# An attention and feed-forward kernel: emission order by measured durations, paced weights, and one weight group more kept in DRAM

## The chip, the cores and the metric

The kernel runs on one core of a Trainium2 chip. The metric is the device time of one execution in microseconds, as the median over several runs. TensorE is PE in the profile, VectorE is DVE, ScalarE is ACT, GpSimd is POOL, and SP is the queue from which nearly all transfers are issued.

## What is computed

Three stages follow one another, over 4 batches of 448 tokens with 768 features:

```
attn = sigmoid(q @ k.T / 8 - log(448));  x = attn @ v          # 12 heads of 64
xk, xr = mu * x + (1 - mu) * x_prev                            # x_prev: one token back
x = sigmoid(xr @ w_r) * (relu(xk @ w_k)**2 @ w_v)              # 768 -> 1024 -> 768
u = x + real(fft over tokens and features of x)
un = (u - mean(u)) / sqrt(var(u) + 1e-6)
out = u + relu(un @ w_ch1) @ w_ch2                             # 768 -> 3072 -> 768
```

## The kernel before

**Precision.** The products of the feed-forward layers are made of three matmuls each: every operand is split into a high and a low part (names that end in `h` and `l`), and high by high, high by low and low by high are added up. The weights arrive as 64-bit floats. `load_split` loads such a piece raw, rebuilds a 32-bit float from its words on DVE (one `ts`, three `stt`, one product), and then writes the high part (a cast) and the low part (a subtraction). In the first stage DVE does all of it, in halves of 128 x 384; a half is seven DVE instructions.

**Stages.** Attention goes by 24 pairs of heads. `scores(i)` makes 7 score products of pair i, `weigh` applies the sigmoid on ACT and writes `sg`, `attnv(i)` multiplies with `v`, and `join` copies the result to `x` (ACT), stores it in DRAM and mixes it with the token before it: `mix` on ACT, `stt` on DVE, a cast to `xkh` on ACT, a subtraction to `xkl` on DVE. Six pairs are one batch. Once a batch's six pieces and the weights `wk` are there, `keys` makes its 8 key tiles of 18 matmuls, between the pairs that are still to come. Behind them lie the receptance (`r`, 4 x 6 tiles of 18 matmuls, on `xr`, the same mix with `mu_r`, read back from DRAM), the values (`v`), into which the Fourier transform of each batch is worked (`pa`, `qa`, `pq`, then a mean `mu` and a variance `var`), and the feed-forward network (`f`): 12 weight groups g by 4 batches, `ffn1(g, b)` 36 matmuls and `ffn2(g, b)` 36. It needs `un`, the split of the centred rows of a batch: `load_k2` makes those of batches 0 and 1, `load_un` those of 2 and 3.

**What sets the order.** Every engine runs its own list in order, and the lists are fixed when the program is built. `Order` keeps a planned clock `o.now` and lets generators emit instructions: each asks in planned time whether what it needs is done (`need`, `issued`), and the cost functions `mm`, `tt`, `stt`, `ts`, `act` and `dma` say how long an instruction is taken to last. These costs move no work and have no effect on the chip but through the order. A key, value or feed-forward matmul waits in `o.feed` and is emitted when no generator is due. `attention` starts a pair every `PACE` us of planned time while there is something in `o.feed`.

**Weights of the first stage.** Two lanes (`first_weights`) start at planned 10 and 13 us, each takes one half of the columns of `wk`, `wr` and the first group of `w1` and `w2`, with one raw buffer. The split first group goes to DRAM (`w0_d`) and comes back by `load_first`. Stage one ends when those stores are issued.

Of the kernel before, what the change touches and what calls it, by code (L numbers as in the profile page):

```python
# [12 lines left out]
F32 = mybir.dt.float32  # L13
# [17 lines left out]
PACE = 11.0  # L31
# [63 lines left out]
class Order:  # L95
# [33 lines left out]

    def run(self, until=None):  # L130

        while until is None or until not in self.at:
# [65 lines left out]
    def stt(self, out, a, scalar, c, op0, op1):  # L198
        self.nc.vector.scalar_tensor_tensor(out, a, scalar, c, op0=op0, op1=op1)  # L199
        return self.spend(self.nc.vector, 0.13 + self.size(out) * 0.00104)  # L200

    def ts(self, out, a, s0, s1, op0, op1):
        self.nc.vector.tensor_scalar(out, a, s0, s1, op0=op0, op1=op1)
        return self.spend(self.nc.vector, 0.07 + self.size(out) * 0.00053)

    def act(self, out, a, fn=None, **kw):
# [4 lines left out]
        return self.spend(self.nc.scalar, 0.05 + self.size(out) * 0.00094)  # L211

    def dma(self, out, src, eng=None):
# [3 lines left out]
        self.free["dma"] = start + b / 4.0 / 220e3  # L217
# [3 lines left out]
def build(tc, ap):  # L221
# [10 lines left out]
    def load_split(pl, parts, gap=0.0, raws=1, lane=0, eng=None, vector=False):  # L232


        def load(src, hi, lo, key):
            n = o.size(hi)
            if not ap["wide"]:
                raw = pl.tile([128, n], F32, tag=f"wst{lane}", name="_".join(map(str, key)), bufs=1)
                return raw, o.dma(raw, src)
# [4 lines left out]
        for i, (wait, src, hi, lo, key) in enumerate(parts):  # L244
            yield from o.issued(*wait)
            raw, t = nxt or load(src, hi, lo, key)
            nxt = None
            ahead = parts[i + 1][1:] if i + 1 < len(parts) and all(k in o.at for k in parts[i + 1][0]) else None
            yield t
            n = o.size(hi)  # L250
# [30 lines left out]
            yield o.now  # L281
# [6 lines left out]
    w0_d = {nm: [dram.tile([128, 2, D], F32, name=f"{nm}0_d{i}") for i in range(2)] for nm in ("w1", "w2")}  # L288
# [39 lines left out]
    def weigh(i, n, ps):  # L328
        sg = att.tile([128, S], F32, tag="sg", name=f"sg_{i}_{n}", bufs=2 * len(places) + 1)
        o.at["sg", i, n] = t = o.act(sg, ps[:, 0:S], AF.Sigmoid, bias=bias_s, scale=1.0 / math.sqrt(DH))  # L330
        sg_t[i, n] = sg
        yield t

    def scores(i):
        k, q = pair_t["k", i], pair_t["q", i]
        for n, (c, j) in enumerate(places):
            ps = ps2.tile([128, 512], F32, tag="sc", name=f"sc_{i}_{n}")
            me = slice(0, 128) if j is None else slice(64 * j, 64 * j + 64)
            o.mm(ps[:, 0:S], k[me, c], q[me], True, True, 0.752 if j is None else 0.376)
            o.spawn(weigh(i, n, ps), o.now + 0.2)  # L340
        o.at["pair", i] = o.now

    def attnv(i, ps):
        v = pair_t["v", i]
        for n in [*range(1, len(places)), 0]:
            c, j = places[n]
            sg = sg_t.pop((i, n))
            if j is None:
                o.mm(ps[:, 0:S], v[:, c].rearrange("p j d -> p (j d)"), sg, False, True, 0.752, skip=True)
            else:  # L350
                me = slice(64 * j, 64 * j + 64)
                o.mm(ps[me, 0:S], v[:, c, j], sg, c == 0, False, 0.376, skip=True)
# [30 lines left out]
    def attention():  # L383
        for i in range(len(pairs) + 1):
            t0 = o.now
            if i < len(pairs):
# [3 lines left out]
                scores(i)  # L390
            if i > 0:
# [3 lines left out]
                attnv(i - 1, bank(f"av_{i - 1}"))  # L395
# [35 lines left out]
    w_parts = [[], []]  # L431
    for f in range(NF + KD):
# [4 lines left out]
        for i in range(2):  # L437
            cs = slice(D // 2 * i, D // 2 * i + D // 2)
            w_parts[i].append(((), src[:, cs], hl[0][:, cs], hl[1][:, cs], (*key, i)))

    def first_weights(lane):

        n = D // 2
        cs = slice(n * lane, n * lane + n)
        yield from load_split(att, w_parts[lane], lane=lane, vector=True)
        for nm in ("w1", "w2"):
            for i in range(2):
                t = att.tile([128, 2, n], F32R, tag=f"first{lane}", name=f"{nm}0_{i}_{lane}", bufs=1)
                yield from load_split(att, [((), ap[nm][i, :, cs], t[:, 0], t[:, 1], ("first", nm, i, lane))], lane=lane, vector=True)
                yield o.at["first", nm, i, lane]  # L450
                o.at["w0_d", nm, i, lane] = o.dma(w0_d[nm][i][:, :, cs], t.bitcast(F32))
# [9 lines left out]
    for i in range(2):  # L461
        o.run(("w0_d", "w2", 1, i))
# [40 lines left out]
    def receptance():  # L503
        for b in range(B):
# [13 lines left out]
    o.spawn(mixes())  # L518
    o.run(("key", B - 1))
# [13 lines left out]
    def load_k2():  # L533
# [10 lines left out]
        for n, (nm, b, i) in enumerate(places):  # L544
            if n >= NK:
# [8 lines left out]
            yield o.now + (0.2 if "receptance" in o.at else 4.0)  # L554
# [13 lines left out]
    o.spawn(load_split(wrp, wv_parts, 0.3, raws=2))  # L568
    o.spawn(receptance())
# [265 lines left out]
    def load_first(nm, pl):  # L835

        ts = w_t[nm, 0] = [
            [pl.tile([128, D], F32R, tag=nm + t, name=f"{nm}{t}0_{i}", bufs=2) for t in "hl"] for i in range(2)
        ]
        for i in range(2):  # L840
            for c, t in enumerate(ts[i]):
                t = o.dma(t.bitcast(F32), w0_d[nm][i][:, c])
            o.at.update(((nm, 0, i, c), t) for c in range(3))

    load_first("w1", wq)
# [12 lines left out]
    def load_un(pl, b):  # L858
# [9 lines left out]
        acc[b] = np_.tile([128, KD, S], F32, tag="x2", name=f"acc{b}", bufs=3)  # L868
# [56 lines left out]
    def out_done(g, b, e, ps):  # L925
        a = acc[b][:, e]
# [60 lines left out]
    load_first("w2", wpa)  # L987
# [7 lines left out]
    acc[1] = unb.tile([128, KD, S], F32, name="acc1")  # L995
# [69 lines left out]
```

## Time and profile before

| what | value |
|---|---|
| three runs | 1284.35, 1282.6, 1283.6 us; median 1283.6 |
| profiled execution, its own time | 1283.99 us |
| its span in the trace | 1282.2 us |
| mean granted clock of TensorE | 0.991 of 2.4 GHz |
| PE busy | 1253.4 us, 98% of the span |
| DVE busy | 737.7 us, 58% |
| ACT busy | 420.4 us, 33% |
| moved by DMA | 157.22 MB, mean 123 GB/s |

The span is that of the trace, 1.8 us shorter than the execution's own time. A row of a timeline has a start in us, a length in us, the engine and line, the operation, and in brackets the idle time before it with what released it. Line numbers are those of the kernel before; those of helpers (L157 for every matmul) say little, so names of tiles are read instead. A float32 product (scores, `av`) counts as two matmul records, and pipelined matmuls overlap in the records.

### The profile page before, as it was taken

To read this page: it belongs to the slowest core of one execution; us is meant where nothing else is said; L and a number is where in the kernel's file an instruction comes from. 1 tells how busy PE (TensorE), PEld (TensorE's weight loads), DVE (VectorE), ACT (ScalarE), POOL (GpSimd) and SP (SyncE) were. 2 spreads that over 40 slices of the span, in tenths; PEclk is the share of its full clock that TensorE was granted. 3 is DMA by queue.
4 is the path that set the end of the run, shared out by engine and by line. 5 is a ranking of instruction groups with operands and counts; after the bars stand their busy time and mean duration, and the time that the engine had idled before them with its cause. 6 is when DMAs were issued, how large, how long until landed. Compare 5 with 4: busy or idle time off the path is not lost.

```text
span 1282.2 us, 15838 instructions
## 1 busy us (share of the span) xinstructions
PE 1253.4 (98%) x6112; PEld 1062.6 (83%) x6112; DVE 737.7 (58%) x1280; ACT 420.4 (33%) x730; POOL 146.1 (11%) x125
## 2 busy tenths in 40 slices
PE   8789999999999999999999999999999999999998
PEld 3246466679888999998999999999999999999998
DVE  4999543123853476787545646564555546565554
ACT  6455666655642112335421212121211112121100
POOL 0000000000000000000111111011111111011486
PEclk9889999999998999999999999999999999999999
DMA  6666765325883644541321202111211112021344
GB/s 202 199 190 195 249 205 179 114 95 189 296 286 131 223 167 161 176 136 68 103 75 50 70 29 75 50 61 38 75 50 50 50 50 75 26 73 50 99 136 160
DMA packets 62763, 157.22 MB, mean 123 GB/s; under 512 B 7584, under 2 KB 33632, under 8 KB 62560
## 3 DMA queue, kind: packets, MB, share of 16 engines
q1 hardware_dynamic: 62016, 153.81, 35.9%
q0 software_dynamic: 672, 2.40, 0.6%
q8 instruction: 48, 0.79, 0.3%
q14 instruction: 27, 0.22, 0.1%
HBM read 113.56 MB, written 42.62 MB: 122 GB/s over the span
## 4 chain that ended last, share of the span: by engine, by line
PE 86%; DVE 10%; ACT 2%; issue 1%; DMA 1%; SPq 0%; DVEq 0%; ACTq 0%
PE f L157 54%; PE k L157 7%; PE v L157 7%; PE r L157 6%; PE sc L157 4%; PE av L157 4%; PE pq L157 1%; DVE wk_bits L199 1%; DVE wr_bits L199 1%; DMA k_d<-kp 1%; DVE x L191 1%; PE qa L157 1%; PE pa L157 1%; DVE wk L199 1%; DVE wk L191 0%
## 5 line engine op out<-in xcount | busy, mean ns | idle before, releaser
L157 PE MATMUL f<-un,w1h 128*128 128x448 f32 x1152 | 329.4, 366 | 1.4 <-DVE un L191 1.4
L157 PEld LDWEIGHTS f<-un,w1h 128*128 128x128 f32 x1152 | 216.5, 188 | 19.5 <-DVE un L191 2.5
L191 DVE TENSOR_TENSOR acc<-acc,f 128x448 f32<-128x448 f32 x264 | 163.0, 619 | 87.7 <-PE f L157 84.8
L157 PE MATMUL f<-hh,w2h 128*128 128x448 f32 x576 | 210.7, 366 | 0.0
L157 PE MATMUL f<-un,w1l 128*128 128x448 f32 x576 | 210.5, 365 | 0.0
L157 PE MATMUL f<-hh,w2l 128*128 128x448 f32 x576 | 210.4, 365 | 0.0
L157 PE MATMUL f<-hl,w2h 128*128 128x448 f32 x576 | 210.4, 365 | 0.0
L199 DVE SCALAR_TENSOR_TENSOR hl<-f,hh 128x448 fp32r<-128x448 f32 x88 | 54.9, 624 | 189.0 <-ACT hh L210 189.0
L210 ACT ACTIVATE hh<-f 128x448 fp32r<-128x448 f32 x88 | 48.0, 546 | 298.0 <-PE f L157 298.0
L157 PEld LDWEIGHTS f<-hh,w2h 128*128 128x128 f32 x576 | 108.2, 188 | 8.8 <-issue 0.2
L157 PEld LDWEIGHTS f<-hl,w2h 128*128 128x128 f32 x576 | 108.2, 188 | 8.7 <-issue 0.2
L157 PEld LDWEIGHTS f<-hh,w2l 128*128 128x128 f32 x576 | 108.2, 188 | 8.6
L157 PEld LDWEIGHTS f<-un,w1l 128*128 128x128 f32 x576 | 108.2, 188 | 8.4
L157 PE MATMUL v<-k,wvh 128*128 128x448 f32 x384 | 112.7, 368 | 0.0
L157 PE MATMUL sc<-q,k 64*128 64x448 f32 (+1 forms) x336 | 94.5, 588 | 18.3 <-ACT sg L210 13.4
L191 POOL TENSOR_TENSOR w1l<-w,w1h 128x768 fp32r<-128x768 f32 x22 | 40.7, 1850 | 511.8 <-ACT w1h L208 294.1
L210 ACT ACTIVATE sg<-sc,bias_s 128x448 f32<-128x448 f32 x168 | 93.7, 642 | 14.6 <-PE sc L157 14.4
L157 PEld LDWEIGHTS sc<-q,k 64*128 64x128 f32 (+1 forms) x336 | 41.6, 194 | 61.2 <-issue 24.9
L157 PE MATMUL av<-sg,v 128*64 128x448 f32 (+1 forms) x336 | 85.8, 577 | 0.0
L199 DVE SCALAR_TENSOR_TENSOR w_bits<-w_raw,w_bits 128x768 uint32<-128x768 uint32 x88 | 84.4, 959 | 1.2
L157 PEld LDWEIGHTS v<-k,wvh 128*128 128x128 f32 x384 | 71.9, 188 | 5.7 <-issue 0.6
L157 PE MATMUL k<-xkh,wkh 128*128 128x448 f32 x192 | 74.8, 390 | 0.0
(138 smaller groups left out, 1640.5 us busy)
## 6 DMA issues: line engine op xcount, KB each, us to landing
w_raw<-in_w SPq DMA_DIRECT2D x44, 768.0 KB, 4.3
k_d<-kp SPq DMA_DIRECT2D x32, 448.0 KB, 3.4
k<-k_d SPq DMA_DIRECT2D x32, 448.0 KB, 5.7
k<-in_k SPq DMA_DIRECT2D x24, 256.0 KB, 3.9
v<-in_v SPq DMA_DIRECT2D x24, 256.0 KB, 3.9
wk_raw<-in_w_k SPq DMA_DIRECT2D x16, 384.0 KB, 3.5
wv_raw<-in_w_v SPq DMA_DIRECT2D x8, 768.0 KB, 6.2
x_d<-x SPq DMA_DIRECT2D x24, 224.5 KB, 3.6
```

The costliest lines, as they stand in the source:

```text
L157: self.nc.tensor.matmul(out, lhs, rhs, start=start, stop=stop, skip_group_check=skip)
L191: eng.tensor_tensor(out, a, c, op=op)
L199: self.nc.vector.scalar_tensor_tensor(out, a, scalar, c, op0=op0, op1=op1)
L210: self.nc.scalar.activation(out, a, fn, **kw)
```

## The change

The cost functions get other constants (matmul, DVE, ACT and DMA), and score and `av` products other fixed costs. `weigh` is no longer spawned for later: it emits its sigmoid right behind its score product. `others` lets every due generator act after each score and `av` product, before the next one is emitted. `PACE` goes from 11.0 to 11.6. The two weight lanes become one, `weights`, which starts at planned 3 us, has two raw buffers, and begins a half no earlier than `EVERY` (6.2 us of planned time) after the one before. The third group that is split in this stage is `w1` of g = 1 (four halves more, 40 instead of 36); `load_early` brings it back, so that the feed-forward stage no longer loads and splits it. `receptance` is spawned before the keys of the last batch are done, and waits for their emission; the split of `wv` is spawned 6 us later; `load_k2` keeps to 8 tiles until the receptance is emitted. `load_un(unc, 2)` is spawned before `network`, not behind the fourth batch's transform, and the accumulators change places.

```diff
-PACE = 11.0
+PACE = 11.6
+EVERY = 6.2
...
+    def others(self):
+        self.hold = True
+        yield self.now
...
-            if self.feed:
+            if self.hold:
+                self.hold = False
+            elif self.feed:
                 self.feed.popleft()()
...
-        self.now += cost or max(0.107, self.size(out) / 2370.0) * (4 if lhs.dtype == F32 else 1)
+        n = self.size(out)
+        self.now += cost or (n / 597.0 if lhs.dtype == F32 else max(0.107, 0.016 + n / 2400.0))
...
-        return self.spend(eng, 0.07 + n * (0.00225 if eng is self.nc.gpsimd else 0.00104))
+        return self.spend(eng, 0.10 + n * (0.00225 if eng is self.nc.gpsimd else 0.00104))
...
-        return self.spend(self.nc.vector, 0.13 + self.size(out) * 0.00104)
+        return self.spend(self.nc.vector, 0.16 + self.size(out) * 0.00104)
...
-        return self.spend(self.nc.vector, 0.07 + self.size(out) * 0.00053)
+        return self.spend(self.nc.vector, 0.18 + self.size(out) * 0.00053)
...
-        return self.spend(self.nc.scalar, 0.05 + self.size(out) * 0.00094)
+        return self.spend(self.nc.scalar, 0.10 + self.size(out) * 0.00094)
...
-        self.free["dma"] = start + b / 4.0 / 220e3
+        self.free["dma"] = start + b / 4.0 / 280e3
...
-            yield o.now
+            if after:
+                o.spawn(after(o.at[key]))
+            yield max(o.now, begun + every)
...
+    EARLY = (("w1", 0), ("w2", 0), ("w1", 1))
...
-            o.mm(ps[:, 0:S], k[me, c], q[me], True, True, 0.752 if j is None else 0.376)
-            o.spawn(weigh(i, n, ps), o.now + 0.2)
+            o.mm(ps[:, 0:S], k[me, c], q[me], True, True, 0.760 if j is None else 0.447)
+            weigh(i, n, ps)
+            yield from o.others()
...
+        yield from load_split(att, w_parts, raws=2, vector=True, every=EVERY)
...
-    for i in range(2):
-        o.spawn(first_weights(i), 10.0 + 3 * i)
+    o.spawn(weights(), 3.0)
...
     def receptance():
+        yield from o.issued(("key", B - 1))
...
     o.spawn(mixes())
+    o.spawn(receptance())
...
+            while n >= NF and "receptance" not in o.at:
+                yield o.now + 0.2
...
-    o.spawn(load_split(wrp, wv_parts, 0.3, raws=2))
-    o.spawn(receptance())
+    o.spawn(load_split(wrp, wv_parts, 0.3, raws=2), o.now + 6.0)
...
+                if (nm, g) in w0_d:
+                    load_early(nm, g, pl)
+                    continue
...
-    load_first("w2", wpa)
+    load_early("w2", 0, wpa)
+    unc = pool(s_l, "unc", 1, "left")
+    o.spawn(load_un(unc, 2))
     o.spawn(network())
...
-    o.spawn(load_un(unb, 2))
-    unc = pool(s_l, "unc", 1, "left")
-    o.spawn(load_un(unc, 3))
+    o.spawn(load_un(unb, 3))
```

The order that follows from it is shown at three places, in the lists of the built programs.

**DVE, attention, pairs 2 and 3.** `mix_k2` and `mix_k3` are the mixes of the third and fourth pair, `wk_4_0` is the first half of the fifth piece of `w_k`. Before, this stands between the two mixes, with one half more (`wk_3_1`, its last two rows are the first ones here) ahead of it:

```order
L276 CAST wkh_174<-wk_3_1_549 128x384
L191 TENSOR_TENSOR wkl_175<-wk_3_1_549,wkh_174 128x384
L203 TENSOR_SCALAR wk_4_0_bits_569<-wk_4_0_raw_508 128x384
L199 SCALAR_TENSOR_TENSOR wk_4_0_bits_569<-wk_4_0_raw_508,wk_4_0_bits_569 128x384 x2
L191 TENSOR_TENSOR wk_4_0_568<-wk_4_0_raw_508 128x384
L199 SCALAR_TENSOR_TENSOR wk_4_0_568<-wk_4_0_568,wk_4_0_bits_569 128x384
L276 CAST wkh_174<-wk_4_0_568 128x384
L191 TENSOR_TENSOR wkl_175<-wk_4_0_568,wkh_174 128x384
L199 SCALAR_TENSOR_TENSOR mix_k3_563<-x_3_527,mu_k_173,mix_k3_563 128x448
L191 TENSOR_TENSOR xkl_2_499<-mix_k2_500,xkh_2_498 128x448
```

After, from one mix to the next:

```order
L209 SCALAR_TENSOR_TENSOR mix_k2_469<-x_2_440,mu_k_175,mix_k2_469 128x448
L201 TENSOR_TENSOR xkl_2_468<-mix_k2_469,xkh_2_467 128x448
L213 TENSOR_SCALAR wk_2_1_bits_514<-wk_2_1_raw_447 128x384
L209 SCALAR_TENSOR_TENSOR wk_2_1_bits_514<-wk_2_1_raw_447,wk_2_1_bits_514 128x384 x2
L201 TENSOR_TENSOR wk_2_1_513<-wk_2_1_raw_447 128x384
L209 SCALAR_TENSOR_TENSOR wk_2_1_513<-wk_2_1_513,wk_2_1_bits_514 128x384
L290 CAST wkh_176<-wk_2_1_513 128x384
L201 TENSOR_TENSOR wkl_177<-wk_2_1_513,wkh_176 128x384
L209 SCALAR_TENSOR_TENSOR mix_k3_533<-x_3_504,mu_k_175,mix_k3_533 128x448
L201 TENSOR_TENSOR xkl_3_532<-mix_k3_533,xkh_3_531 128x448
```

Before, two halves lie between two mixes and the subtraction of a pair stands behind the next pair's mix; now each pair has its mix, its subtraction and one half.

On PE the keys begin at the same place in both, behind the eighth group of scores. Before they follow in runs of 1 to 47 matmuls; now the list is 8 groups of scores and 7 of `av`, and then 16 times 24 key matmuls, a group of scores and a group of `av` in turn, and 192 key matmuls at the end.

**ACT, receptance, third batch (`r_2_e`) and the mixes for the fourth (`mix_r3_p`, `xrh_3_p`).** Before, the last two pieces of the fourth batch stand here:

```order
L210 ACTIVATE r_2_4_3387<-r_2_4_3345 128x448
L210 ACTIVATE mix_r3_3_3397<-xr_3_3_3232,mu_r_2523 128x448
L208 CAST xrh_3_3_3234<-mix_r3_3_3397 128x448
L210 ACTIVATE r_2_5_3415<-r_2_5_3385 128x448
L210 ACTIVATE wv_5_3422<-wv_5_raw_3275 128x768
L208 CAST wvh_2785<-wv_5_3422 128x768
L210 ACTIVATE mix_r3_4_3431<-xr_3_4_3360,mu_r_2523 128x448
L208 CAST xrh_3_4_3362<-mix_r3_4_3431 128x448
L210 ACTIVATE mix_r3_5_3436<-xr_3_5_3375,mu_r_2523 128x448
L208 CAST xrh_3_5_3377<-mix_r3_5_3436 128x448
```

After:

```order
L220 ACTIVATE r_2_2_3393<-r_2_2_3354 128x448
L218 CAST wvh_2856<-wv_4_3310 128x768
L220 ACTIVATE wv_5_3412<-wv_5_raw_3308 128x768
L220 ACTIVATE r_2_3_3423<-r_2_3_3391 128x448
L220 ACTIVATE mix_r3_4_3434<-xr_3_4_3361,mu_r_2574 128x448
L218 CAST xrh_3_4_3363<-mix_r3_4_3434 128x448
L220 ACTIVATE r_2_4_3454<-r_2_4_3421 128x448
L220 ACTIVATE mix_r3_5_3460<-xr_3_5_3383,mu_r_2574 128x448
L218 CAST wvh_2856<-wv_5_3412 128x768
L218 CAST xrh_3_5_3385<-mix_r3_5_3460 128x448
```

The mix of piece 4 moved from behind `r_2_5` to behind `r_2_3`, that of piece 5 to behind `r_2_4`, and the split of `wv` that stood ahead of piece 4 begins earlier.

**DVE, behind the mean of the fourth batch.** `x2_3` is the fourth batch, `un_2_i` and `un_3_i` are the split rows of the third and fourth. Before:

```order
L191 TENSOR_TENSOR un_2_3_5405<-x2_2_4148,un_2_3_5405 128x448
L191 TENSOR_TENSOR sum_v_3_5443<-sum_v_3_5443,sq_3_5465 128x448 x2
L191 TENSOR_TENSOR x2_3_4562<-x2_3_4562,mu_3_5371 128x448 x2
L199 SCALAR_TENSOR_TENSOR w1_1_0_2_bits_5476<-w1_1_0_2_raw_5400,w1_1_0_2_bits_5476 128x768
L191 TENSOR_TENSOR un_3_2_5411<-x2_3_4562,un_3_2_5411 128x448
L191 TENSOR_TENSOR un_2_4_5406<-x2_2_4148,un_2_4_5406 128x448
L191 TENSOR_TENSOR un_3_3_5412<-x2_3_4562,un_3_3_5412 128x448
L199 SCALAR_TENSOR_TENSOR w1_1_0_2_bits_5476<-w1_1_0_2_raw_5400,w1_1_0_2_bits_5476 128x768
L191 TENSOR_TENSOR un_2_5_5407<-x2_2_4148,un_2_5_5407 128x448
L191 TENSOR_TENSOR sum_v_3_5443<-sum_v_3_5443,sq_3_5515 128x448 x2
L191 TENSOR_TENSOR un_3_4_5413<-x2_3_4562,un_3_4_5413 128x448
L191 TENSOR_TENSOR un_3_5_5414<-x2_3_4562,un_3_5_5414 128x448
```

After:

```order
L201 TENSOR_TENSOR un_3_0_5520<-x2_3_4609,un_3_0_5520 128x448
L201 TENSOR_TENSOR un_3_1_5521<-x2_3_4609,un_3_1_5521 128x448
L201 TENSOR_TENSOR sum_v_3_5546<-sum_v_3_5546,sq_3_5563 128x448 x2
L201 TENSOR_TENSOR x2_3_4609<-x2_3_4609,mu_3_5489 128x448 x2
L201 TENSOR_TENSOR un_3_2_5522<-x2_3_4609,un_3_2_5522 128x448
L209 SCALAR_TENSOR_TENSOR hl_0_2_5578<-f1_0_2_0_5541,hh_0_2_5577 128x448
L201 TENSOR_TENSOR un_3_3_5523<-x2_3_4609,un_3_3_5523 128x448
L201 TENSOR_TENSOR sum_v_3_5546<-sum_v_3_5546,sq_3_5596 128x448 x2
L201 TENSOR_TENSOR un_3_4_5524<-x2_3_4609,un_3_4_5524 128x448
L209 SCALAR_TENSOR_TENSOR hl_0_2_5578<-f1_0_2_1_5571,hh_0_2_5577 128x448
L213 TENSOR_SCALAR w2_1_0_2_bits_5619<-w2_1_0_2_raw_5518 128x768
L201 TENSOR_TENSOR un_3_5_5525<-x2_3_4609,un_3_5_5525 128x448
```

The rows of the third batch are gone from here (they stand ahead of the fourth batch's transform), and the first raw word operation is now for `w2`. On PE the mean's product comes later: behind it, 11 matmuls are left to the first one of `ffn1(0, 2)` and 47 to the first of `ffn1(0, 3)`, where there were 42 and 78.

## Rows read from the trace of the kernel before

**Rows 1.** the page's first part: busy time, share of the span and instructions

```profile
PE 1253.4 (98%) x6112; PEld 1062.6 (83%) x6112; DVE 737.7 (58%) x1280; ACT 420.4 (33%) x730; POOL 146.1 (11%) x125
```

**Rows 2.** stretches: span; busy PE, PEld, DVE, ACT, POOL (counts); granted clock; DMA share, GB/s

```profile
14.65:31.43 16.78, 16.78 (x71) 6.69 (x71) 8.81 (x18) 12.45 (x23) 0.20 (x2) 1.00 0.58 177
31.43:147.00 115.57, 101.97 (x407) 54.18 (x405) 105.16 (x217) 62.94 (x118) 1.19 (x9) 0.93 0.65 203
56.00:64.00 8.00, 8.00 (x20) 2.76 (x20) 7.65 (x17) 4.02 (x8) 0.00 (x0) 0.63 0.63 190
388.00:409.00 21.00, 21.00 (x94) 19.42 (x95) 8.62 (x11) 5.87 (x9) 0.00 (x0) 0.88 0.27 93
408.90:562.30 153.40, 152.92 (x870) 141.67 (x869) 101.55 (x230) 32.08 (x62) 2.94 (x5) 1.00 0.52 177
616.00:1282.00 666.00, 662.63 (x3270) 613.85 (x3269) 363.46 (x539) 126.93 (x188) 138.37 (x91) 1.00 0.21 68
```

**Rows 3.** waits of PE over the whole span: total us, times, longest us

```profile
PE sc L157 <- ACT sg L210: 13.4, 5, 7.7
PE r L157 <- ACT xrh L208: 4.2, 3, 3.7
PE f L157 <- DVE un L191: 1.4, 2, 1.1
PE r L157 <- DVE xrl L191: 0.8, 2, 0.6
```

**Rows 4.** chain that ended last, pieces in order of time: start us, us, what

```profile
4.62 10.03 PE sc L157 x28
14.65 3.35 PE av L157 x14
18.01 3.44 PE sc L157 x14
...
280.88 31.41 PE k L157 x155
...
338.69 36.89 PE r L157 x182
```

**Rows 5.** timelines of DVE, ACT and PE, 50 to 59 us: start, length, what [idle before]

```profile
50.05 0.35 DVE L203 TENSOR_SCALAR wk_bits<-wk_raw 128x384 uint32<-128x384 uint32 x1
53.56 0.68 DVE L199 SCALAR_TENSOR_TENSOR mix_k<-x,mu_k,mix_k 128x448 f32<-128x448 f32 x1
...
54.27 0.56 ACT L208 CAST xkh<-mix_k 128x448 fp32r<-128x448 f32 x1 [7.04 <-DVE mix_k L199]
54.74 0.53 ACT L208 COPY x<-av 128x448 f32<-128x448 f32 x1
55.16 3.79 ACT L210 ACTIVATE sg<-sc,bias_s 128x448 f32<-128x448 f32 x7
58.81 0.70 ACT L210 ACTIVATE mix_k<-x,mu_k 128x448 f32<-128x448 f32 x1
...
55.86 2.38 PE L157 MATMUL sc<-q,k 64*128 64x448 f32 x4 [7.73 <-ACT sg L210]
```

**Rows 6.** timelines of ACT, DVE and PE, 379 to 386 us

```profile
379.29 0.55 ACT L210 ACTIVATE r<-r 128x448 f32<-128x448 f32 x1 [1.22 <-PE r L157]
383.15 0.96 DVE L191 TENSOR_TENSOR wvl<-wv,wvh 128x768 fp32r<-128x768 f32 x1 [0.90 <-ACT wvh L208]
385.35 0.48 PE L157 MATMUL r<-xrh,wrh 128*128 128x448 f32 x1 [3.75 <-ACT xrh L208]
```

**Rows 7.** timeline of DVE behind the fourth batch's mean

```profile
595.12 1.15 DVE L191 TENSOR_TENSOR x<-x,mu 128x448 f32<-128x448 f32 x2 [2.46 <-PE mu L157]
```

**Rows 8.** DMA issues: shape of the transfer, count, KB each, median us to landing

```profile
w_raw<-in_w SPq DMA_DIRECT2D x44, 768.0 KB, 4.3
wk_raw<-in_w_k SPq DMA_DIRECT2D x16, 384.0 KB, 3.5
w1l<-w_d SPq DMA_DIRECT2D x2, 384.0 KB, 11.7
```

More of the change, by code (lines that the diff above doesn't have):

```diff
@@ L230, in pool, with load_split @@
         return stack.enter_context(tc.tile_pool(name=name, bufs=bufs, side=side, reuse_waits="tile"))
-    def load_split(pl, parts, gap=0.0, raws=1, lane=0, eng=None, vector=False):
+    def load_split(pl, parts, gap=0.0, raws=1, lane=0, eng=None, vector=False, every=0.0):
         def load(src, hi, lo, key):
-            n = o.size(hi)
+            n = o.size(src)
             if not ap["wide"]:
-                raw = pl.tile([128, n], F32, tag=f"wst{lane}", name="_".join(map(str, key)), bufs=1)
+                raw = pl.tile([128, n], F32, tag=f"wst{lane}", name="_".join(map(str, key)), bufs=raws)
                 return raw, o.dma(raw, src)
@@ L245, in load_split @@
             yield from o.issued(*wait)
+            begun = o.now
             raw, t = nxt or load(src, hi, lo, key)
@@ L249, in load_split @@
             yield t
+            after = None
+            if callable(hi):
+                hi, lo, after = hi()
             n = o.size(hi)
@@ L287, in build @@
     u_d = [dram.tile([128, KD, S], F32, name=f"u_d{b}") for b in range(B)]
-    w0_d = {nm: [dram.tile([128, 2, D], F32, name=f"{nm}0_d{i}") for i in range(2)] for nm in ("w1", "w2")}
+    EARLY = (("w1", 0), ("w2", 0), ("w1", 1))
+    w0_d = {(nm, g): [dram.tile([128, 2, D], F32, name=f"{nm}_{g}_d{i}") for i in range(2)] for nm, g in EARLY}
     c_d = [dram.tile([128, KD, S], F32, name=f"c_d{b}") for b in range(2)]
@@ L389, in attention @@
                     yield from o.need(("sg", i - 1, 2))
-                scores(i)
+                yield from scores(i)
             if i > 0:
@@ L438, in build, with weights, first, store @@
             cs = slice(D // 2 * i, D // 2 * i + D // 2)
-            w_parts[i].append(((), src[:, cs], hl[0][:, cs], hl[1][:, cs], (*key, i)))
-    def first_weights(lane):
+            w_parts.append(((), src[:, cs], hl[0][:, cs], hl[1][:, cs], (*key, i)))
+    def weights():
         n = D // 2
-        cs = slice(n * lane, n * lane + n)
-        yield from load_split(att, w_parts[lane], lane=lane, vector=True)
-        for nm in ("w1", "w2"):
+        def first(nm, g, i, c):
+            t = att.tile([128, 2, n], F32R, tag="first", name=f"{nm}_{g}_{i}_{c}", bufs=2)
+            def store(when):
+                yield when
+                o.at["w0_d", nm, g, i, c] = o.dma(w0_d[nm, g][i][:, :, n * c : n * c + n], t.bitcast(F32))
+            return t[:, 0], t[:, 1], store
+        for nm, g in EARLY:
             for i in range(2):
[L448 to L451, printed above, removed]
+                for c in range(2):
+                    src = ap[nm][2 * g + i, :, n * c : n * c + n]
+                    w_parts.append(((), src, partial(first, nm, g, i, c), None, ("first", nm, g, i, c)))
+        yield from load_split(att, w_parts, raws=2, vector=True, every=EVERY)
     load_mu(mu_k, ap["mu_k"])
@@ L553, in load_k2 @@
                 o.spawn(split(t, ("un", b, i), V), o.dma(t[:, 1].bitcast(F32), c_d[b][:, i]))
-            yield o.now + (0.2 if "receptance" in o.at else 4.0)
+            yield o.now + (0.2 if "receptance" in o.at else 5.0)
     def load_r():
@@ L833, in build, with load_early @@
     w_t = {}
-    def load_first(nm, pl):
-        ts = w_t[nm, 0] = [
-            [pl.tile([128, D], F32R, tag=nm + t, name=f"{nm}{t}0_{i}", bufs=2) for t in "hl"] for i in range(2)
+    def load_early(nm, g, pl):
+        ts = w_t[nm, g] = [
+            [pl.tile([128, D], F32R, tag=nm + t, name=f"{nm}{t}{g}_{i}", bufs=2) for t in "hl"] for i in range(2)
         ]
@@ L925, in out_done @@
     def out_done(g, b, e, ps):
+        while b not in acc:
+            yield o.now + 0.1
         a = acc[b][:, e]
```

26 lines of the change are left out of this document (13 added, 13 removed).

## The prediction

> **What bounds the kernel now.** I read the page's first part first: PE is busy 1253.4 of 1282.2 us [rows 1], so the whole kernel offers at most 28.8 us of idle PE, and whatever is cheaper on DVE or ACT counts only where PE stood still or ran slowly. The stretches then say where that is [rows 2]. From 616 us to the end PE is busy 662.63 of 666.00 us at a granted clock of 1.00, and from 408.9 to 562.3 us (the values and most of the transforms) 152.92 of 153.40: nothing is to be had there. From 31.43 to 147 us it is busy 101.97 of 115.57 at 0.93, with DVE busy 105.16: there the idle time and the slow time lie. From 388 to 409 us the clock is 0.88. The list of PE's waits names the causes: score products that wait for ACT's sigmoid, 13.4 us in 5 waits; receptance products that wait for the split mix, 4.2 and 0.8; feed-forward products that wait for the centred rows, 1.4 [rows 3].
>
> The timelines of the three engines show how the longest of these waits arises [rows 5]. DVE starts a weight half at 50.05 and comes to `mix_k` only at 53.56, 3.5 us later. The cast `xkh` on ACT needs that mix; it stands in ACT's list ahead of the next seven sigmoids and lets ACT idle for 7.04 us. PE, which needs the sigmoids to free its banks, idles 7.73 us, and from 56 to 64 us its granted clock is 0.63, near the lower of its two levels (1.2 of 2.4 GHz) [rows 2]. So a pair of heads waits for weights it does not need yet, because two or three halves stand in DVE's list ahead of its mix.
>
> **Change, part 1: attention and keys.** In the new order DVE has one half between two mixes, and a pair's subtraction follows its own mix. The sigmoids stand directly behind their score products. What DVE does per pair is then one half, 3.5 us, a mix, 0.68, and a subtraction, about 0.6 (taken as half of the row with two subtractions of that size, 1.15 [rows 7]): 4.8 us. ACT does seven sigmoids in 3.79, a copy 0.53, a mix 0.70 and a cast 0.56 [rows 5]: 5.6 us. PE has 3.44 us of scores and 3.35 of `av` per pair [rows 4]: 6.8 us, and from the seventh pair on also 24 key matmuls at 31.41 / 155 = 0.203 us [rows 4], so 11.7 us. PE is the slowest of the three in both stretches; the stretch 14.65 to 31.43, where the same groups ran with PE busy 16.78 of 16.78 us at clock 1.00, shows that they can follow each other without idle time [rows 2]. If they do so throughout, the end of the keys follows. Two groups of scores are done at 14.65 us, as before [rows 4]; there remain 22 groups of scores, 24 of `av` and all 576 key matmuls (32 tiles of 18):
>
> 14.65 + 22 x 3.44 + 24 x 3.35 + 576 x 0.2026 = 14.65 + 75.7 + 80.4 + 116.7 = 287.4 us.
>
> Before, the keys ended at 280.88 + 31.41 = 312.3 [rows 4]. **Gain: 24.9 us.** Two checks of what could be late. The first keys stand behind the eighth group of scores and the seventh of `av`: 14.65 + 6 x 3.44 + 7 x 3.35 = 58.7 us. They need the sixth pair's cast and subtraction, whose `av` ends one group of each, 6.8 us, earlier at 51.9; copy, mix, DVE's mix, cast and subtraction are 0.53 + 0.70 + 0.68 + 0.56 + 0.6 = 3.1, and at worst a half (3.5) stands ahead: 58.5. The piece is used last in each tile, so it is there. At the end, 192 key matmuls follow the last `av`, 144 of them of the last batch; the 48 ahead take 9.7 us, against 3.1 to 6.6 for the last pair's mix. The half stands ready in a second raw buffer, and its load (3.5 us [rows 8]) lies beside DVE's work.
>
> The bounds: nothing is gained at all if the waits only move (0), and no more than the 24.9, as the sum leaves PE no idle time. I take the upper end, since both other engines have 1 us or more to spare per pair, and correct it below by a small sum.
>
> **Part 2: receptance.** Its 24 tiles of 18 are 432 matmuls; at 36.89 / 182 = 0.2027 us [rows 4] they need 87.6 us. Before they lasted from 312.3 to 408.9, where the next stretch begins [rows 2], 96.6 us. **Gain: 9.0 us.** The waits are 5.0 of it [rows 3]; the 21 us at 0.88 [rows 2] are 21 x 0.12 = 2.5; the remaining 1.5 are matmuls that overlap less around those stalls. The stall has its row: ACT is at 379.29 with the third batch's sigmoid, DVE writes the `wv` split at 383.15 after waiting for ACT, and PE waits 3.75 us for the last `xrh` [rows 6]. In the new list the mixes of pieces 4 and 5 of the fourth batch stand behind `r_2_3` and `r_2_4`, one tile (18 x 0.2027 = 3.65 us) or two earlier. The sigmoid of `r_2_4` can start 17 tiles after the stage's start, at 62.0; then 0.55, a mix 0.70, DVE's mix 0.68, a `wv` cast of about 0.96 (the DVE row of the same shape [rows 6]) and the `xrh` cast 0.56: about 65.5, a subtraction 66.1. The first tile of the fourth batch starts after 18 tiles, 65.7, and needs its sixth piece 15 matmuls later, at 68.7. The margin is some 2.5 us: enough, but the thinnest in this stage. If it is missed, up to the old 9.0 comes back.
>
> **Part 3: the centred rows.** `load_un` of the third batch goes ahead of the network, so only six `un_3` remain behind the fourth mean. Before, PE waited 1.4 us there [rows 3]; **gain 1.4**. But the cover on PE shrinks too: from the mean's product to the first product that needs `un_3` it is 47 matmuls, and its last piece comes 15 later: 62 x 0.2027 = 12.6 us. DVE has about 20 instructions to do before `un_3_5`; at 1.15 / 2 [rows 7] they take 11.5. Margin 1.1. One of them is the first operation on a raw `w2` piece, whose load is queued on SP behind four loads of the group brought back from DRAM. At the median of 4.3 us for a raw piece it is hidden; at the 11.7 us of a `w1l` load from DRAM [rows 8] it is 7.4 later, which would make PE wait at the start of the fourth batch. I work that case out as 11.7 - 4.3 = 7.4, less the 4.6 us of the 8 DVE instructions that can go ahead and the margin of 1.1: 1.7 us.
>
> **Part 4: costing nothing.** The split of `w1` for g = 1 moves from the feed-forward stage, where PE has no idle time, to DVE's idle part behind the keys; the four halves are 14 us of DVE work, its stores and loads 4 x 384 KB more or less of 157 MB. The number of matmuls is unchanged. That cover is gone only if the halves delay the receptance's mixes: rival E. The cost constants themselves do nothing but set the order.
>
> The sum is 24.9 + 9.0 + 1.4 = 35.3 us. The profiled execution took 1284.0, so it would become 1248.7; the median is 0.4 lower: 1248.3. For the small waits of new neighbours I add 0.7 (half of the F term; an estimate): **1249.0 us**.
>
> **Rivals.**
> A. *A third of the attention loss stays*, for example because DVE's half still meets the `xkl` of some pairs. For: DVE is busy 105.16 of 115.57 us there [rows 2], and it has the same halves to do. Against: one half per 6.8 us of PE leaves it 2.0 us. Price 8.3: 1257.
> B. *The receptance's stall returns* since the margin of 2.5 us is missed. For: `wv` casts still stand among the mixes. Against: they are one tile earlier. Price 9.0: 1258.
> C. *The fourth batch's rows or the raw `w2` come late*: 1.7 us, 1250 to 1251. It lies within the forecast's own range.
> D. *The clock falls*. The first 44 us after 14.65 hold short groups only, with banks handed from PE to ACT and back. If PE's short stops between groups kept the clock at the 0.93 of the old stretch, 44 us / 0.93 would be 3.3 more: 1252; at 0.63 [rows 2], 44 / 0.63 = 26 more: 1275. Against it stands the row at 14.65 to 31.43: same groups, 1.00 [rows 2]. The Trainium skill, "TensorE: Matmul & The Clock Gate", section "A second HAM failure mode: psum-queue depth-cycling", tells of a kernel whose clock went up and down because PE paused briefly between groups while it cycled its banks. By that page the change could bring such a stretch; the row with the same groups speaks against it.
> E. *One lane is too slow: slower.* 40 halves now go through a single lane, where two lanes had 36. If a load of 3.5 us [rows 8] and a conversion of 3.5 us [rows 5] ran one after the other, with a pause of 0.5, a half would take 7.5 us, the 40 would end at 5 + 300 = 305 us (5 as the first products begin at 4.62 [rows 4]), and the reload of `xr` and its mixes (about 24 us, an estimate: six pieces by 3.5, as for a half's load, and one mix chain of 3.1) would let the receptance begin at 329 instead of 287.4: 42 us later, 1291. It decides from about 7.3 us a half (5 + 40 x 7.3 + 24 is 34 later), where the 35 us are gone. Against: two buffers let load and conversion overlap, so DVE's 3.5 and the pace of 6.2 set the time.
>
> **How the numbers follow.** Forecast with C 0.70, A 0.10, B 0.10, D 0.05 (half of it below 1258), E 0.03; the remaining 0.02 is no effect at all. The forecast's own range is 1245.6 to 1252: 3.4 us below, if the little idle time of the last stretch (666.00 less 662.63 [rows 2]) went as well, since DVE splits one group less there; 3 above for C and for small new waits. To reach 8 in 10 the range must take in A, and B, equally likely, lies 1 us beyond: 1245.6 to 1258. A measurement of this kernel can tell 0.2%, 2.6 us, from no change. Faster holds for the forecast, A, B and nearly all of D: 0.94; within 0.2% 0.03; slower, E, 0.03.
>
> **What would show it.** Right: from 31 to 147 us PE idle for under 2 us with clock 1.00; DVE's timeline there with one half per pair; keys ending near 287 us; the last receptance product near 375; no wait of `r` for `xrh` above 0.5 us; waits of `f` for `un` under 2 us; the stretch from the fourth mean to the end as long as before. Wrong: a wait of `sc` for `sg` of several us, or of `k` for `xkl` (part 1); a wait of `r` for `xrh` or `wrh` (part 2, E); a clock below 1.00 between 15 and 60 us without such a wait (D). A new wait in the feed-forward stage for `w1h` or `w1l` of g = 1, which now come from DRAM, would be a loss that I have put at nothing.

## The result and the profile after

| | before | changed |
|---|---|---|
| median of four runs | 1283.84 us | 1252.9 us (1252.1 to 1253.45) |
| ratio, 95% interval | | 0.976 (0.9743 to 0.9777) |
| span | 1282.2 | 1251.0 |
| last key product starts | 311.9 | 291.1 |
| first value product starts | 408.8 | 378.2 |
| from there to the end of the span | 873.4 | 872.8 |

The time fell by 30.9 us. The forecast was 1249.0, with a range of 1245.6 to 1258; it was worked out from the median of three runs, 1283.6, and the table has a fourth. The last three rows divide the 31.2 us of the spans: 20.8 came in attention and keys, 9.7 in the receptance (96.8 us from the last key product to the first value product, against 87.1), 0.7 behind it. Here and below, differences are taken before rounding.

First the busy line of the changed kernel, which answers to [rows 1]:

```profile
PE 1240.2 (99%) x6112; PEld 1058.9 (85%) x6112; DVE 743.1 (59%) x1300; ACT 418.8 (33%) x726; POOL 141.8 (11%) x123
```

DVE has more to do than before and the kernel is shorter: PE's idle and slow time went. Its waits, in total, times and longest, answer to [rows 3]:

```profile
PE sc L166 <- DMA q<-in_q: 4.8, 1, 4.8
PE f L166 <- DVE un L201: 0.9, 2, 0.5
PE v L166 <- DMA k<-k_d: 0.8, 1, 0.8
PE f L166 <- DVE hl L209: 0.3, 1, 0.3
```

The first is the start of the program. No wait of `sc` for `sg` and none of `r` is left. The stretches (span; busy PE, PEld, DVE, ACT, POOL with counts; granted clock; DMA share, GB/s) show attention, the receptance, the values with transforms, and the last stage:

```profile
31.43:147.00 115.57, 115.57 (x499) 64.19 (x499) 80.19 (x160) 78.41 (x147) 1.33 (x12) 1.00 0.59 193
...
291.50:378.40 86.90, 86.90 (x434) 80.99 (x433) 55.46 (x78) 45.98 (x78) 0.00 (x0) 1.00 0.71 243
378.40:531.20 152.80, 151.99 (x870) 140.58 (x869) 99.35 (x227) 31.51 (x62) 2.94 (x5) 1.00 0.54 187
...
587.85:1251.00 663.15, 659.18 (x3253) 610.65 (x3252) 356.63 (x532) 126.06 (x185) 136.25 (x90) 1.00 0.20 67
```

The first row is the same window as the second of [rows 2]: 499 products instead of 407, no idle time, clock 1.00 instead of 0.93, and DVE at 80 us instead of 105. DVE's timeline has one weight half between two mixes there (the subtraction at 48.05 is the half's last step), and DVE waits for ACT's mix instead of being late with its own:

```profile
42.53 0.68 DVE L209 SCALAR_TENSOR_TENSOR mix_k<-x,mu_k,mix_k 128x448 f32<-128x448 f32 x1 [0.72 <-ACT mix_k L220]
44.47 0.62 DVE L201 TENSOR_TENSOR xkl<-mix_k,xkh 128x448 fp32r<-128x448 f32 x1 [1.26 <-ACT xkh L218]
...
48.05 0.56 DVE L201 TENSOR_TENSOR wkl<-wk,wkh 128x384 fp32r<-128x384 f32 x1
49.33 0.68 DVE L209 SCALAR_TENSOR_TENSOR mix_k<-x,mu_k,mix_k 128x448 f32<-128x448 f32 x1 [0.73 <-ACT mix_k L220]
```

What is missing against the forecast stands in the chain that ended last (start, length, what), where the keys begin:

```profile
62.30 3.35 PE av L166 x14
65.65 4.86 PE k L166 x24
70.51 3.95 PE sc L166 x14
74.46 3.35 PE av L166 x14
77.81 4.86 PE k L166 x24
82.67 3.44 PE sc L166 x14
86.11 3.35 PE av L166 x14
89.46 4.86 PE k L166 x24
94.32 4.06 PE sc L166 x14
```

Key and `av` groups take what the prediction took. A score group takes 3.44 us, but 4.06 each third time: five groups with 0.62 more, the first with 0.51, and small parts make 3.9 us. In ACT's timeline at the group of 94.32, two steps of a key tile's eviction, `kt`, stand between the first and second sigmoid:

```profile
95.11 0.64 ACT L220 ACTIVATE sg<-sc,bias_s 128x448 f32<-128x448 f32 x1 [2.32 <-PE sc L166]
95.64 0.54 ACT L220 ACTIVATE kt<-k 128x448 f32<-128x448 f32 x1
96.21 0.58 ACT L220 ACTIVATE kt<-kt 128x448 f32<-128x448 f32 x1
96.69 2.19 ACT L220 ACTIVATE sg<-sc,bias_s 128x448 f32<-128x448 f32 x4
```

A tile ends after 18 products and a block has 24, so a tile ends with a block each third time, and its eviction falls into the scores.

### The profile page after: what moved, and what is told of

It reads as the page before. It is cut to its first block, busy times and chain, and to the rows that moved or that the text cites. A ratio compares the mean times of both kernels' runs of the same rounds, so it can differ in the third digit from the quotient of the medians.

```text
span 1251.0 us, 15841 instructions
## 1 busy us (share of the span) xinstructions
PE 1240.2 (99%) x6112; PEld 1058.9 (85%) x6112; DVE 743.1 (59%) x1300; ACT 418.8 (33%) x726; POOL 141.8 (11%) x123
## 4 chain that ended last, share of the span: by engine, by line
PE 97%; DVE 1%; DMA 1%; issue 0%; SPq 0%; DVEq 0%
PE f L166 55%; PE k L166 9%; PE v L166 8%; PE sc L166 7%; PE r L166 7%; PE av L166 6%; PE pq L166 1%; PE pa L166 1%; PE qa L166 1%; DMA k<-k_d 1%; DVE un L201 1%; PE var L166 0%; DVE x L201 0%; PE mu L166 0%; DMA q<-in_q 0%; PE sp L166 0%
## 5 line engine op out<-in xcount | busy, mean ns | idle before, releaser
L201 POOL TENSOR_TENSOR w2l<-w,w2h 128x768 fp32r<-128x768 f32 x22 | 40.9, 1859 | 384.4 <-ACT w2h L218 313.0
L209 DVE SCALAR_TENSOR_TENSOR w_bits<-w_raw,w_bits 128x768 uint32<-128x768 uint32 x84 | 81.8, 973 | 1.5
L166 PE MATMUL av<-sg,v 128*64 128x448 f32 (+1 forms) x336 | 82.2, 554 | 0.0
```

## The experiments

My theory M: halves of weights ahead of a pair's mix were the loss of the attention stage, so the paced lane is the gain. Rival S: what helps is that the sigmoids stand directly behind their products. Then the same for the receptance: the placing, or something else. The code cuts show the main lines of each edit. All results (median us; ratio, with its 95% interval, to runs of the kernel before that were taken beside it; start of the last key product and of the first value product; from there to the end of the span):

| kernel | median | ratio | last key | first value | rest |
|---|---|---|---|---|---|
| two_lanes | 1324.68 | 1.0326 (1.031 to 1.0341) | 363.6 | 450.7 | 873.7 |
| lane_alone | 1278.64 | 0.9951 (0.9936 to 0.9966) | 299.9 | 403.5 | 873.4 |
| sig_later | 1284.77 | 1.0013 (1.0004 to 1.0022) | 300.2 | 411.1 | 872.8 |
| no_hold | 1279.96 | 0.9971 (0.996 to 0.9982) | 288.9 | 405.0 | 873.0 |
| every0 | 1254.27 | 0.9772 (0.9756 to 0.9788) | 293.2 | 380.3 | 872.2 |
| costs_alone | 1329.37 | 1.0365 (1.0347 to 1.0382) | 361.1 | 448.2 | 878.0 |
| rec_old | 1252.68 | 0.9763 (0.9748 to 0.9777) | 290.7 | 377.9 | 872.5 |
| rec_both | 1262.87 | 0.9836 (0.9821 to 0.9851) | 290.1 | 386.5 | 872.7 |
| rec_costs | 1257.81 | 0.98 (0.9785 to 0.9814) | 291.4 | 385.2 | 871.9 |
| un_late | 1257.24 | 0.9797 (0.9783 to 0.9812) | 291.6 | 378.7 | 877.9 |
| early_two | 1254.61 | 0.9778 (0.9763 to 0.9793) | 291.6 | 378.7 | 875.5 |
| keys_aside | 1248.66 | 0.9732 (0.9717 to 0.9746) | 287.6 | 374.7 | 872.4 |

**two_lanes.**

```diff
...
-    o.spawn(weights(), 3.0)
+    for i in range(2):
+        o.spawn(first_weights(i), 10.0 + 3 * i)
...
```

> The changed kernel with its single paced weight lane put back to the two unpaced lanes with one raw buffer each; all else as changed, the three early groups too. DVE's list then has two to ten weight halves between the mixes of neighbouring pairs. Theory M (halves ahead of a mix hold the pair, and through the cast on ACT the sigmoids): PE waits for the sigmoids again and the time is 1268 to 1285 us. Rival S (what helps is that each sigmoid stands directly behind its score product, so that ACT's list no longer blocks): no more than 1258 us.

It came out far worse than either theory's range. PE's waits, and the stretch in which they lie:

```profile
PE sc L166 <- ACT sg L220: 65.9, 4, 38.0
...
31.43:142.00 110.57, 44.65 (x143) 16.09 (x141) 104.27 (x217) 27.08 (x51) 1.33 (x6) 0.69 0.53 165
```

Here twelve halves, 12 x 3.5 = 42 us, stand between two mixes, and the wait of 38 us lies in them. The two mixes on DVE, and the cast on ACT behind the second, which the next sigmoids stand behind:

```profile
81.75 0.68 DVE L209 SCALAR_TENSOR_TENSOR mix_k<-x,mu_k,mix_k 128x448 f32<-128x448 f32 x1
...
124.94 0.68 DVE L209 SCALAR_TENSOR_TENSOR mix_k<-x,mu_k,mix_k 128x448 f32<-128x448 f32 x1
125.65 0.57 ACT L218 CAST xkh<-mix_k 128x448 fp32r<-128x448 f32 x1 [39.42 <-DVE mix_k L209]
```

PE is busy for 44.65 of 110.57 us, at a granted clock of 0.69. The direction of M is shown, its size was far too small, and the sigmoids' place does not protect against it.

**costs_alone.** The constants of the cost functions, in the kernel before, with the one other line of the change that `out_done` waits until its accumulator is there.

```diff
...
-        self.free["dma"] = start + b / 4.0 / 220e3
+        self.free["dma"] = start + b / 4.0 / 280e3
...
```

> The kernel before with the new cost constants alone (matmul, DVE, ACT, DMA, fixed costs of score and value products); PACE stays 11.0, two lanes, all placing as before. The faster planned DMA lets the lanes place up to seven halves between two mixes, where there were two or three. Theory M: slower than before, 1286 to 1300 us. Rival (truer costs make a better order by themselves): 1265 to 1282 us.

Slower, as M has it, but by 46 us instead of 2 to 16. Its PE waits 64.7 us for sigmoids, in three waits, as with two_lanes. "Truer" constants alone made unpaced lanes run further ahead of the pairs: in the trace sixteen halves lie between the mixes at 69.80 and 127.54, where the expectation had up to seven. The rest of the kernel is 4.5 us longer too, with 5.1 us of waits for `un` instead of 1.4. But the receptance took 448.2 - 361.1 = 87.1 us here, with the old placing.

**lane_alone.**

```diff
...
-    for i in range(2):
-        o.spawn(first_weights(i), 10.0 + 3 * i)
+    o.spawn(weights(), 3.0)
...
```

> The kernel before with the single paced lane alone (start at planned 3 us, two raw buffers, a half every 6.2 us, two early groups as before); costs, sigmoids and everything behind as before. Mostly one or two halves between two mixes. Theory M: most of the attention term comes, 13 to 20 us: 1264 to 1271 us. Rival S: the sigmoids still stand behind the casts, so 1278 us or more.

By the time M misses, and S's "1278 us or more" holds by 0.6. By the stages it is nearer to M: the keys end 12.0 us earlier than before, one short of its 13 to 20, and the receptance gives 6.7 back, by three short waits at its start and the stall of the old order, now 5.9 us. PE's waits in the whole run, the sigmoids' share among them:

```profile
PE r L158 <- ACT xrh L209: 8.1, 4, 5.9
PE sc L158 <- ACT sg L211: 4.8, 2, 3.0
```

**sig_later.** The sigmoids spawned for later, the pause gone, and the old fixed costs of score and value products.

```diff
-            weigh(i, n, ps)
-            yield from o.others()
...
+            o.spawn(weigh(i, n, ps), o.now + 0.2)
...
```

> The changed kernel with score and value products emitted as before: seven products in one go, their sigmoids spawned for later, with the old fixed costs of these products. The paced lane stays, and DVE has one or two halves between mixes. Theory M: 1253 to 1258 us. Rival S: 1264 us or more, with waits of score products for sigmoids.

M misses: 1284.77, and S's range and its sign hold, the sign weakly: score products wait 5.5 us for sigmoids, in six waits. The keys end 9.0 us later than in the changed kernel. The larger part, 23.8 us, is lost behind them, where PE waits once more, 14 us for `xrh`. What is late there is the lane. SP's timeline has its last raw load, its last store and the first loads of `xr`:

```profile
300.48 0.47 SPq L224 DMA_DIRECT2D first_w_raw<-in_w  x1
...
308.26 0.52 SPq L224 DMA_DIRECT2D w_d<-w  x1
308.88 0.56 SPq L224 DMA_DIRECT2D mu_r<-in_mu_r  x1
309.49 4.77 SPq L224 DMA_DIRECT2D xr<-x_d  x5
```

Stage one ends when the last store is issued, and `xr` is loaded behind it. So the receptance cannot start before weights have been split that are first used some 250 us later. In the changed kernel the same row lies 29 us ahead of the receptance:

```profile
261.54 0.52 SPq L224 DMA_DIRECT2D w_d<-w  x1
262.15 0.56 SPq L224 DMA_DIRECT2D mu_r<-in_mu_r  x1
262.76 0.51 SPq L224 DMA_DIRECT2D xr<-x_d  x1
```

**no_hold.** The pause alone is taken out; the sigmoids keep their place.

```diff
             weigh(i, n, ps)
-            yield from o.others()
...
```

> The changed kernel without the pause after each score and value product, in which every due generator emits; the sigmoids still stand directly behind their products. DVE's list then has two mixes, two subtractions and two halves in turn, and ACT two mixes and two casts together, behind seven sigmoids. Theory M2 (a pair's mix must come with its pair, as the banks and the tiles of x are few): PE waits for sigmoids or for xkl, 1256 to 1266 us. Rival (the sigmoids' place alone does it): 1252.5 to 1255 us.

It separates the two effects. The attention stage is better than in the changed kernel: PE busy 115.57 of 115.57 us, the last key product at 288.9 instead of 291.1. All that is lost, and more, is lost at the receptance's start. The stretch, PE's longest wait and SP's last rows of the lane:

```profile
31.43:147.00 115.57, 115.57 (x501) 65.34 (x501) 73.32 (x144) 80.24 (x149) 1.69 (x13) 1.00 0.61 198
...
299.27 4.30 SPq L224 DMA_DIRECT2D w_d<-w  x2
...
309.19 0.74 PE L166 MATMUL r<-xrh,wrh 128*128 128x448 f32 x1 [19.92 <-ACT xrh L218]
```

M2 as I wrote it is refuted, since mixes in twos behind seven sigmoids cost PE nothing; the rival's 1252.5 to 1255 is missed as well. The run also gives S its share: sig_later differs from no_hold only in the place of the sigmoids and in the fixed costs of the score and value products, and its last key product starts 11.3 us later. Which of the two makes it, no run separates. The pause matters since it keeps the lane at its pace: from its first load at 2.60 to its last subtraction the lane takes 6.47 us a half in the changed kernel (to 261.5, 40 halves) and 7.5 here (to 303.0). That the lane falls behind because a planned half can then only begin between whole groups is my reading of the code; it was not tried with another pace.

**every0.**

```diff
-EVERY = 6.2
+EVERY = 0.0
```

> The changed kernel with the pace of the halves off (0 instead of 6.2 us): one lane, two raw buffers, a half as soon as the one before is planned done. DVE's list has one or two halves between two mixes, nine in the first six pairs where there were seven. If it is the single lane that matters, 1252.5 to 1256 us. If it is the pace, the mixes wait behind two halves of 3.5 us and PE for the sigmoids: 1258 to 1275 us.

The single lane (with its two raw buffers and its earlier start) is what matters; the pace is worth 1.4 us by the medians, with intervals that overlap; what shows of it lies in attention (last key product 2.1 later, two waits for sigmoids of 0.5 in all). The lane's last subtraction is done at 195.5, far from the receptance.

**rec_old.** The receptance's edits undone.

```diff
     def receptance():
-        yield from o.issued(("key", B - 1))
...
-    o.spawn(load_split(wrp, wv_parts, 0.3, raws=2), o.now + 6.0)
+    o.spawn(load_split(wrp, wv_parts, 0.3, raws=2))
+    o.spawn(receptance())
```

> The changed kernel with the receptance stage's edits undone: it is spawned behind the keys, the split of w_v with no delay, and the load of k2 goes on at its old pace. The attention stage is as changed. If the placing is what removes the stall (term of 9.0 us), waits of r for xrh or xrl come back and the time is 1259 to 1263 us. Rival: the stall is gone because of the costs or the earlier keys, 1252 to 1255 us.

The placing has no effect. That leaves the constants or the lighter load, which the next two separate.

**rec_both** and **rec_costs.** The old constants between the end of attention and the end of the receptance, with the old and with the new placing.

```diff
+    o.old = True
...
     o.run("receptance")
+    o.old = False
```

> The changed kernel with the receptance placed as before and, for the stretch from the end of the attention stage to the end of the receptance alone, the old cost constants. ACT's list there has the order of the kernel before: mixes of pieces 4 and 5 of the fourth batch behind r_2_5. Theory K (the constants made the order that removed the stall, not the placing): waits of r for xrh return, 1258 to 1263 us. Rival L (the stall went because DVE and the queues are less loaded once the keys end earlier): 1252 to 1254.5 us.

> The changed kernel with the old cost constants in the same stretch, and the new placing kept. ACT's list has the last two mixes behind r_2_5 and one split of w_v more ahead of them. Theory K: waits of r for xrh, 1257 to 1264 us. Rival P (the placing suffices, either half of the edit does): 1252 to 1254.5 us.

Theory K holds in both. In rec_both ACT's order is that of before, and so is the stall; PE's row of it and the stretch behind it:

```profile
363.55 0.74 PE L167 MATMUL r<-xrh,wrh 128*128 128x448 f32 x1 [3.75 <-ACT xrh L222]
...
365.00:387.00 22.00, 21.88 (x97) 19.68 (x97) 9.39 (x12) 6.55 (x11) 0.05 (x1) 0.88 0.26 89
```

This is the wait of [rows 6] again, to a hundredth, and the clock of 0.88 of [rows 2]. With the old constants the new placing takes half of the stall's waits away (2.5 us are left of 4.6) and 2.6 of the 9.2 us by which the stretch from the last key product to the first value product is too long; with the new constants it makes no difference which placing is used, and the stall is gone. Rival L has costs_alone against it too: there the keys end 49 us later than before, not earlier, and the stall is gone.

**un_late.**

```diff
...
-    unc = pool(s_l, "unc", 1, "left")
-    o.spawn(load_un(unc, 2))
...
-    o.spawn(load_un(unb, 3))
+    o.spawn(load_un(unb, 2))
+    unc = pool(s_l, "unc", 1, "left")
+    o.spawn(load_un(unc, 3))
```

> The changed kernel with the third batch's centred rows placed as before, behind the fourth batch's transform, and the accumulators with them. By my term F PE waits 1.4 us more for un: 1253.5 to 1254.5 us. Rival: the matmuls in the feed between cover it, 1252.9 us within 0.4.

More than either: 4.3 us. Its waits behind the fourth mean (one of 0.21 stands ahead of them), the stretch around them, and the same window of the changed kernel:

```profile
577.02 0.47 PE L166 MATMUL f<-un,w1h 128*128 128x448 f32 x1 [0.38 <-ACT un L218]
579.56 0.47 PE L166 MATMUL f<-un,w1h 128*128 128x448 f32 x1 [2.06 <-DVE un L201]
580.63 0.47 PE L166 MATMUL f<-un,w1h 128*128 128x448 f32 x1 [0.19 <-DVE un L201]
...
568.70:590.20 21.50, 18.66 (x79) 15.60 (x78) 16.10 (x28) 12.90 (x24) 0.00 (x0) 0.92 0.39 143
568.70:590.20 21.50, 21.50 (x106) 19.67 (x105) 15.81 (x31) 10.68 (x19) 0.00 (x0) 1.00 0.44 157
```

PE is idle for 2.84 us there, the short wait of 0.21 included, and the clock of 0.92 over 21.5 us is 1.7 more: 4.6 in all. The changed kernel has no idle time there.

**early_two.**

```diff
-    EARLY = (("w1", 0), ("w2", 0), ("w1", 1))
+    EARLY = (("w1", 0), ("w2", 0))
```

> The changed kernel with two early groups instead of three: w1 of g = 1 is loaded and split in the feed-forward stage again, four halves fewer behind the keys. As PE has no idle time to win in the feed-forward stage, 1252.9 us within 0.6. Rival: the group in DRAM frees the raw w2 load at the fourth batch, so without it PE waits there and it is 1254 us or more.

The rival, if barely: 1.7 us slower by the medians, with intervals that overlap. In its trace PE has one wait more at the fourth batch:

```profile
588.10 0.47 PE L166 MATMUL f<-un,w1h 128*128 128x448 f32 x1 [1.06 <-DVE un L201]
```

and 1.1 us more of waits for `k2` in the values (1.9 instead of 0.8). Only the first has to do with the edit by what the trace shows; the second varies from kernel to kernel between none (keys_aside) and 1.9.

**keys_aside.**

```diff
+    def clear():
+        while o.scoring:
+            yield o.now + 0.1
...
     def key_done(b, f, ps):
...
+        yield from clear()
         o.act(t, ps, AF.Relu)
...
```

(`scoring` is true while a group of seven scores is being emitted. The same wait stands ahead of the other two ACT steps.)

> The changed kernel, where the three ACT instructions that evict a key tile (two kt, one kp) are kept from being emitted while a group of seven scores is. If they are what stretches every third score group from 3.44 to 4.06 us (the sigmoids stand behind two kt of 0.55 us), the keys end 3.1 to 3.9 us earlier: 1249 to 1250 us. If the long groups come from something else (a weight load, a DMA of k or q), 1252.4 to 1253.5 us.

It is the fastest kernel here, 4.2 us below the changed one (the intervals overlap at their ends, but its slowest run, 1249.37, is faster than the changed kernel's fastest, 1252.1; the spans agree, 1247.1 against 1251.0). Its chain at the place of the long score group, and ACT's timeline there:

```profile
89.08 4.86 PE k L167 x24
93.94 3.44 PE sc L167 x14
97.38 3.35 PE av L167 x14
...
94.73 0.64 ACT L221 ACTIVATE sg<-sc,bias_s 128x448 f32<-128x448 f32 x1 [2.31 <-PE sc L167]
95.68 3.26 ACT L221 ACTIVATE sg<-sc,bias_s 128x448 f32<-128x448 f32 x6 [0.31 <-PE sc L167]
98.79 0.58 ACT L221 ACTIVATE kt<-k 128x448 f32<-128x448 f32 x1
```

All seven sigmoids come first, `kt` behind them, and the group takes 3.44 us. The last key product starts at 287.6, 3.5 us earlier, and the span is 3.9 shorter.

## Why the prediction was right, and where it was not

**What bounds the kernel** held: all of the gain lies where the profile of before had idle or slow PE, and the values and the feed-forward stage together are within 0.7 us of before.

**Part 1** forecast 24.9 us and 20.8 came. The step that was mis-sized is ACT's sum per pair, "seven sigmoids in 3.79, a copy 0.53, a mix 0.70 and a cast 0.56": it left out the eviction of the key tiles, two `kt` and a `kp` of 0.55 to 0.58 us each. On the average they fit (1.7 us for each 18 key products), but they stood among the sigmoids in each third group. keys_aside takes them out of the score groups, and the receptance's first product then starts at 287.8, against 287.4 in the sum.

One check of this part counted wrongly, and so does the text on PE's list ahead of the prediction. In the traces the first keys stand behind nine groups of scores and eight of `av`, at 65.65 in the changed kernel (its `av` group at 62.30 is the eighth), not behind eight and seven at 58.7. In the sum for the end of the keys each group is counted once, so it is not touched; the check's margin, 58.5 against 58.7, was in truth about 7 us.

The mechanism was half of the story. With twelve or sixteen halves ahead of a mix the loss is large (two_lanes, costs_alone), and a single lane removes it even without a pace (every0). But the other edits are needed too. Without the pause the attention stage is as fast and the lane is late, which I had only as rival E; and with the sigmoids spawned for later, at the old fixed costs, the keys end 11.3 us later than in no_hold.

**Part 2** forecast 9.0 and 9.7 came, from the order that the text named, the mixes of the last two pieces ahead of `r_2_4` and `r_2_5`. My expectation that the placing of the receptance made that order was wrong; the constants did (rec_old, rec_both, rec_costs). "The cost constants themselves do nothing but set the order" was true, and that was all of this term.

**Part 3** forecast 1.4, and 0.7 came from the whole rest. The medians cannot settle such a difference, but the waits say where it went. Behind the fourth mean no wait is left, so the 1.4 of [rows 3] came in full. New are the 0.9 of waits for `un` and the 0.3 for `hl` in the list above, which lie ahead of the fourth mean:

```profile
534.96 0.47 PE L166 MATMUL f<-un,w1h 128*128 128x448 f32 x1 [0.50 <-DVE un L201]
542.30 0.47 PE L166 MATMUL f<-un,w1h 128*128 128x448 f32 x1 [0.39 <-DVE un L201]
```

At the second of them DVE's timeline has subtractions of the third batch between those of an earlier one. In un_late, where the third batch's rows come later, that wait and the one for `hl` are gone, and the first stays. So the earlier rows have a price of 0.7 us, a term that the prediction put at nothing without a reason. Its worry, that fewer products cover the rows, did not come true; and with the third batch's rows left late the loss is 4.3 us, three times the term.

**Part 4** put the third early group at nothing. Without it PE waits 1.1 us more for the fourth batch's rows (early_two), though the medians do not settle that the time is longer; that it is the raw load and DVE's work on it that meet those rows is likely from the order, and no run separates it.

**Rivals.** A took place, at half of its price, by another cause than DVE. B and C did not. D did not: PE was busy for all of the stretch from 31.43 to 147 us in groups that cycle through five score banks, and the granted clock was 1.00. The Trainium skill, "TensorE: Matmul & The Clock Gate", section "A second HAM failure mode: psum-queue depth-cycling", tells of another kernel in which PE paused between groups and the clock went up and down. Here PE did not pause, so this row neither confirms nor refutes it. E did not happen in the changed kernel, whose lane ends 29 us early, but it is real: at 7.5 us a half in no_hold, close to the 7.3 that the prediction gave as the point where the gain is gone, the time was 1279.96. The start of the receptance was estimated for such a case at 329 us and was 309.2. The estimate of 24 us for loads and mixes was the part that failed: from the lane's last subtraction at 303.0 to the first product it took 6 us, as SP issues five of the six loads within 4.6 us.

## What to carry to other kernels

When an engine's list is fixed in advance, an early piece of work that nobody waits for yet does harm by standing ahead of a small piece that others do wait for: read which instruction the waiting engine names, and then what stands ahead of it in the list of the engine before. Work of a later stage that must end before a stage can close needs its own end time in the plan, with its slack known (29 us here; in the two kernels where the lane was late it ended 8 and 14 us behind the keys). Every periodic piece of work counts in an engine's budget twice, by its mean and by where its phase puts it: 1.1 us of evictions cost nothing on the average and 0.6 us in each third group.

## What the runs showed of the hardware

After an idle time of PE of 3.75 us, in rec_both, the next 14 products took from 363.55 to 370.0 us, first 0.4 to 0.7 us apart and then 0.37, where they are 0.20 apart otherwise; the granted clock of that stretch was 0.50, the lower of the two levels (1.2 of 2.4 GHz). With 4.6 us of waits for the split mix, the stretch from the last key product to the first value product was 9.2 us longer than in the changed kernel (96.3 against 87.1). In un_late 2.5 us more of waits went with a rest that was 5.1 us longer in the trace, 4.3 by the medians. In two_lanes, where one wait was 38 us long, 65.9 us of waits made the keys end 72.5 us later. What came on top of the waits was thus 4.6, 2.6 and 6.6 us: in these three runs it did not grow in proportion to their length, so short waits cost about twice their length and long ones hardly more than it. I had not expected that.
